# A new written-out order of all steps in a fused attention and gated-MLP kernel, and its PE fillers

## Chip, cores, metric

One core of one Trainium2 chip. The metric is device time in microseconds (us) of one execution, lower is better; what is given is the median of three runs.

## What is computed

Attention in chunks of 32 positions over 8 memory keys and a context of up to 56 neighbours, then a gated MLP with a spatial mix over the sequence:

```python
# q, k, v: 4 batches, 8 heads, 768 positions, 64 wide
for c in range(24):                                   # chunks of 32
    scores = scale * q_c @ concat(mem_k, k_ctx).T     # 8 + up to 56 keys
    a = softmax(scores)
    out[c] = a @ concat(mem_v, v_ctx)
x = out as (4, 768, 512)
h = gelu(x @ w_in)                                    # 512 -> 1024
u, v = halves of h
v_n = (v - mean) / sqrt(var + 1e-6) * g_ln
v_s = w_sg @ v_n + b_sg                               # over the 768 positions
y = x + (u * v_s) @ w_out                             # 512 -> 512
```

## The kernel before

The whole kernel is some 1,100 small named steps. Each is defined once (`step(name, does, engine)`, line 184) and issued by the loop at lines 490 to 495 in the order of the names in the table `ORDER` (line 31). Every engine's wrapper (`InOrder`, line 86) keeps program order, so that `ORDER` is at once the order of each engine's queue and that of the DMA issues, which all stand on SP's queue. A star behind a name takes the step's second engine. No planner runs here: what stands in the table is what happens.

The steps, by their names:
- `q`, `k`, `v` + unit: loads of an attention unit. A unit (0 to 23) is 128 positions of one batch with all 8 heads; q and k have two buffers, v three.
- `S` + unit (line 285): the scores, 32 matmuls of 64x32 by 64x64 in float32 into one of two PSUM halves. Then on DVE `mx` (row maximum), `sb` (subtract), on ACT `ex` (exp), on DVE `sm`, `sa`, `sr` (sum, add, reciprocal) and on DVE or POOL `nm` (normalise).
- `T` + unit (line 327): four 128x128 transposes; `p` copies them to SBUF (ACT or DVE).
- `A` + unit (line 341): attention times values, 32 float32 matmuls; `xc`, `xh`, `xl` copy the result and split it into a high and a low float32r part (ACT, then DVE or POOL).
- `ri`, `ro`, `d1` to `d9` (line 190): the weights w_in (8 pieces, half 1 before half 0) and w_out (4 pieces) arrive as 64-bit numbers and are turned into high and low parts on DVE, ACT and POOL; `g`, `ga`, `gb` do the same for w_sg from float32.
- `V` + batch and unit within the batch (line 396): the v half of x @ w_in for 128 positions, 12 matmuls of 128x128 by 128x512 (3 products of high and low parts over 4 blocks of 128). Then `v1` (gelu, ACT), `v5`, `vx`, `vy`, `v6` (statistics), `v7`, `v8`, `v9` (normalise and split).
- `U` + batch, half (384 positions) and block (line 431): 12 matmuls by 128x384 and the gelu `u1`. A `U` of half 0 needs the units 0 to 2 of its batch and the first four pieces of w_in's half 0.
- `W` (line 438): the spatial mix, 18 matmuls, needs all six `v9` of the batch; `w1`, `w2` shift and gate on DVE, `w3`, `w4` split again.
- `O` (line 456): 12 matmuls with w_out, needs four `w4` and the w_out parts; `o1` adds x, `out` stores.
- `zz` + n: n filling matmuls of 128x128 on the identity into a free PSUM tile (`warm`, line 486); nothing reads them.

PE's products go to one of four PSUM tiles (mma to mmd), taken at the matmul and given back by the step that reads them. So the S and A steps of the units, 48 in all and needed by the V and U steps of their batch, are spread between the large products. Batch 0 is the start-up: its V, U and W come in the first 125 us, while the weights are still being made. From 200 us on the order is nearly all large products.

Of the kernel before, what the change touches and what calls it, by code (L numbers as in the profile page):

```python
# [32 lines left out]
zz8 q2 sb0 d9i11 mx1 ex0 k2 z0 sb1 sm0 ex1 sa0 sm1 k3 sr0 sa1 nm0 sr1 d2i12 q3 T0 nm1 d4i12 p0* T1 ri03 d2i13 p1
A0 d1i12 d4i13 d1i13 d6i12 A1 zz9 d3i12 ri01 d6i13 d3i13 d5i12 xh0 xh1 d5i13 v3 xc0 d2i10 xc1 d7i13 xl0 d4i10 v4
d1i10 d8i13 d6i10 g11 d3i10 d9i13* d7i12* S2 zz2 g30 d5i10 d8i12 mx2 g41 d7i10 xl1 S3 zz3 k4 d9i12 sb2 d8i10 mx3
ex2 q4 d9i10* sb3 V01 sm2 ex3 q5 d1i03 sa2 d1i01 d3i03 sr2 sm3 nm2* d3i01 k5 V00 d1i00 sa3 d5i01 ri02 v101 sr3
d2i00 g31 nm3 d3i00 g21 d4i00 d2i03 d5i00 g20 T3 d4i03 T2 d6i00 p3 g40 p2* d7i00 v100 A3 g10 d6i03 d8i00 S4 ro0
d2i01 xc3 d9i00 v501 A2 d4i01 v6 mx4 xh3 d6i01 S5 zz2 xh2 xl3 sb4 xc2 q6 xl2 k7 mx5 d7i01 V02 q7 ex4 k6 d2i02
d8i01 v5 d1i02 sm4 d4i02 cb d9i01* d3i02 d6i02 V03 sa4 d5i02 sr4 sb5 d7i02 v102 nm4 vx01 d5i03 T4 ex5 p4* d8i02
z5 d7i03* A4 d9i02 sm5 d8i03 vy01 S7 v502 xc4 v7 sa5 v601 S6 xh4 d9i03* k9 sr5 q9 xl4 mx7 ga41 U000 k8 ga40 mx6  # L40
q8 ga11 nm5* sb7 ga10 ga20 sb6 ex7 gb10 U001 ex6 v701 ga21 g00 ga30 gb40 sm7 v801 vx02 V04 ga31 gb30* z6 g51
gb41 sa7 gb31 sm6 g50 u1001 sr7 vy02 sa6 nm7* u1000 S9 v901* v602 T5 k11 S8 p5 q11 gb11 sr6 mx9 v104 k10 U003
nm6 ga00 q10 ga51 gb21 mx8 g01 ga50 sb9 gb00 sb8 T7 v504 T6 gb20 ex9 A5 p6 v702 ex8 gb50 sm9 S11 v8 xc5 p7* S10
v802 q13 sm8 xh5 k13 v902 A7 mx11 k12 ga01 q12 A6 xl5* v10 gb01 u1003 v9 U010 xc6 sa8 sb11 xc7 sr8 v103 sa9 vx04
nm8 sr9 U013 vy04 mx10 nm9* ex11 gb51* v604 sb10 z11 V05 sm11 v704 u1010 sa11 v500 sr11 d2o0 vx00 nm11* vy00
v503 ex10 T9 T8 v600 v804 p9* S12 p8 sm10 v904 d4o0 S13 k14 mx12 q14 A9 sa10 mx13 k15 q15 v700 A8 v12 sb13 u1013
v105 vx03 sr10 sb12 v800 nm10* v11 U002 vy03 v505 v603 d6o0 vx05 v703 ex13 T11 vy05 v900* ex12 v605 T10 p11* S14
v803 z12 xc9 v705 S15 k16 xc8 v903 mx14 q16 v805 U011 mx15 k17 p10 sm12 q17 v905 sb15 sa12 sm13 W013 u1002 sr12
d1o0 nm12* sa13 sb14 ex15 d3o0 sr13 sm15 ex14 W010 nm13 d5o0 sa15 sm14 d7o0 ro1 u1011 sr15 w1013 nm15* d8o0 W000
sa14 d9o0 w2013 sr14 w1010 nm14 d2o1 d1o1 d4o1 w2010 W012 d3o1 w1000 d6o1 d5o1 w2000 d7o1 ro2 w3000 w4000* T13  # L50
d8o1 T12 w1012 S17 d9o1* S16 mx17 q19 k19 A11 mx16 q18 sb17 k18 A10 xc11 v14 sb16 d2o2 v13 W001 p12* d1o2 ex17
d3o2 z17 sm17 d4o2 d5o2 xc10 p13 U012 sa17 d6o2 ex16 sr17 w1001 d7o2 ro3 nm17 d8o2 W002 w2001 w3010 d9o2* w4010
sm16 u1012 sa16 d1o3 w3001 d2o3 d3o3 w2012 T15 T14 d4o3 w4001* T17 d5o3 w3012 A12 w3013 w1002 w4013 A13 p14 v15
w4012* S19 p15 v16 w2002 d6o3 S18 w3002 q21 mx19 w4002 k21 W003 q20 mx18 k20 sb19 sb18 ex19 d7o3* ex18 sr16 d8o3
z18 nm16* W011 sm18 w1003 d9o3 sa18 w2003 sm19 w3003 S21 sr18 w4003 w1011 S20 q23 nm18 k23 O003 w2011 k22 mx21
q22 w3011 mx20 w4011* O001 sb21 o1003 ex21 sa19 out003 sr19 sm21 nm19* O000 sa21 o1001 sr21 out001 nm21* O010
o1000 out000 O013 o1010 out010 O012 o1013 out013 O011 o1012 out012 O002 o1011 xh11 xh10 out011 xl11* xh9 xl10
V15 o1002 xh7 xl9 xh6 out002 xh8 xl7* xl6* V11 xl8* v115 xc12 xc13 U103 v111 v511 vx11 vy11 v611 U111 u1103 v711
v811 v911* V14 u1111 V10 v114 v514 vx14 vy14 v614 v714 A14 v110 v814 v510 T18 xc14 v17 v914 T16 vx10 vy10 T19
sb20 S23 v610 p16* S22 ex20 mx23 A15 sm20 mx22 A16 xc15 v18 p17* sb22 A17 p18 v19 sa20 v710 ex22 sr20 sb23 v20  # L60
V13 nm20* p19 sm22 xc17 xc16 sa22 sr22 v810 nm22 ex23 v910 U112 z23 sm23 v113 v513 U100 u1112 sa23 vx13 sr23
vy13 nm23 v613 v713 v813 T20 T22 u1100 v913 T21 A18 A19 p20* v21 p21* v22 V12 U101 v112 v512 vx12 vy12 v515 v612
U102 u1101 v712 v812 vx15 vy15 v615 v912* U110 u1102 v715 v815 v915* U113 u1110 W102 u1113 W100 w1102 w2102
w3102 w4102* W101 w1100 w2100 w3100 w4100 W103 w1101 w2101 w3101 w4101* W111 w1103 w2103 w3103 w4103 W113 w1111
w2111 w3111 w4111 W110 w1113 w2113 w3113 w4113* O100 w1110 w2110 w3110 w4110* O103 o1100 out100 W112 o1103
out103 O102 w1112 w2112 w3112 w4112 O101 o1102 out102 O111 o1101 xh14 xh12 out101 xl14 xh13 xl12* O110 o1111
xl13 out111 xc19 xc18 O112 o1110 out110 V21 o1112 out112 O113 v121 v521 vx21 vy21 v621 V20 o1113 xh17 v721 xh16
out113 xl17* xh15 xl16* v821 xl15 V24 v120 v921* v520 vx20 vy20 v620 V22 v124 v720 v524 v820 vx24 v920 vy24 V25
v624 v122 v724 v522 v824 vx22 v924* vy22 v622 U211 v125 v722 v525 v822 vx25 v922* U212 u1211 vy25 v625 v725 v825
A20 u1212 v925* A21 xc20 p22* v23 xc21 V23 U201 v123 v523 vx23 vy23 v623 U200 u1201 v723 v823 v923* U203 u1200  # L70
W210 u1203 W203 w1210 U202 w1203 w2203 U213 u1202 w3203 w4203* W202 u1213 U210 w1202 w2202 w3202 w4202* W212
u1210 w2210 w3210 w4210* W211 w1212 w2212 w3212 w4212 W213 w1211 w2211 w3211 w4211 W200 w1213 w2213 w3213 w4213*
W201 w1200 w2200 w3200 w4200* T23 w1201 A22 p23 w2201 A23 w3201 xc22 w4201 xc23 O213 O202 o1213 out213 O201
o1202 out202 O211 o1201 out201 O203 o1211 out211 O200 o1203 out203 O212 o1200 xh19 xh20 out200 xl19 xh18 xl18*
O210 o1212 xl20 out212 V31 o1210 xh23 xh21 out210 xl23* xh22 xl21 xl22* V32 v131 v531 vx31 vy31 v631 v731 V33
v132 v831 v532 v931 vx32 vy32 v632 U310 v133 v732 v832 v932* V35 u1310 U303 v135 v535 vx35 vy35 v635 V34 u1303
v735 v835 v935* V30 v134 v534 vx34 vy34 v634 v734 U313 v130 v834 v530 v934 vx30 vy30 v533 U300 u1313 v630 v730
v830 vx33 vy33 U301 v633 u1300 v930* v733 v833 U311 v933 u1301 W301 u1311 W303 w1301 w2301 W313 w1303 w2303 U302
w1313 w2313 U312 u1302 w3303 w3301 w4303* w4301* W300 w3313 u1312 w4313 W311 w1300 w2300 w3300 w4300 W312 w1311
w2311 w3311 w4311 W302 w1312 w2312 w3312 w4312* W310 w1302 w2302 w3302 w4302* O301 w1310 w2310 w3310 w4310 O302  # L80
o1301 out301 O310 o1302 out302 O313 o1310 out310 O311 o1313 out313 O312 o1311 out311 O300 o1312 out312 O303
# [477 lines left out]
```

## Time and profile before

| | us |
|---|---|
| median of three runs (lowest, highest) | 414.51 (411.21, 415.73) |
| the profiled execution's own time | 411.95 |
| its span, first to last instruction | 410.0 |
| granted clock of PE, mean of the span | 0.971 |

| engine | busy us | share | instructions |
|---|---|---|---|
| PE (matmuls) | 381.1 | 93% | 4862 |
| DVE | 223.7 | 55% | 440 |
| ACT | 160.1 | 39% | 267 |
| POOL | 101.6 | 25% | 112 |

Busy time is what an engine's instructions cover. PE's weight loads (PEld) stand in a row of their own and run beside its matmuls. A wait called "issue" is idle time for which the profile shows no other engine or transfer that ended it. Every step is recorded through one helper, so all rows have its line, L94; steps are told apart by the names of their tiles.

### The profile page before, as it was taken

How to read it: one execution, taken by the hardware profiler on the slowest of the kernel's cores; microseconds unless marked ns; L12 is line 12 of the kernel's file. 1: busy time of each engine (PE TensorE's matmuls, PEld its weight loads, DVE VectorE, ACT ScalarE, POOL GpSimd, SP SyncE). 2: the span in 40 equal slices, each digit the busy share in tenths (PEclk: the TensorE clock that was granted, in tenths of full speed). 3: DMA queues.
4: the chain of work that ended last, by engine and by line, in shares of the span. 5: the costliest groups of instructions: out<-in, count | busy, mean ns of one | idle time of the engine just before them, and what ended most of it. 6: DMA issues, size and time to landing. Idle time of an engine off the chain costs nothing.

```text
span 410.0 us, 10958 instructions
## 1 busy us (share of the span) xinstructions
PE 381.1 (93%) x4862; PEld 357.5 (87%) x4862; DVE 223.7 (55%) x440; ACT 160.1 (39%) x267; POOL 101.6 (25%) x112
## 2 busy tenths in 40 slices
...
GB/s 285 407 395 243 190 235 202 230 112 245 64 270 76 212 199 77 2 73 137 105 1 2 6 71 74 5 54 0 0 2 2 98 58 2 0 0 2 0 62 93
DMA packets 19151, 43.96 MB, mean 107 GB/s; under 512 B 2592, under 2 KB 8224, under 8 KB 19104
## 3 DMA queue, kind: packets, MB, share of 16 engines
...
q8 instruction: 38, 0.62, 0.6%
...
HBM read 36.96 MB, written 6.29 MB: 105 GB/s over the span
## 4 chain that ended last, share of the span: by engine, by line
PE 87%; DVE 4%; issue 4%; ACT 2%; DMA 2%; SPq 0%
PE mmc L94 21%; PE mma L94 21%; PE mmd L94 18%; PE mmb L94 16%; PE av L94 6%; PE s L94 4%; DMA kb<-in_ks 2%; DVE ea L94 1%; SPq L94 0%; DVE paira L94 0%; DVE eb L94 0%; ACT L94 0%; DVE w_in_lo L94 0%; ACT pt L94 0%; ACT xa L94 0%
## 5 line engine op out<-in xcount | busy, mean ns | idle before, releaser
...
L94 DVE SCALAR_TENSOR_TENSOR mmd<-mmd,g_all,b_all 128x384 f32<-128x384 f32 x10 | 6.2, 624 | 21.2 <-PE mmd L94 21.2
L94 PE MATMUL s<-kb,qb 64*32 64x64 f32 x768 | 11.5, 232 | 6.6 <-issue 5.2
L94 PEld LDWEIGHTS s<-kb,qb 64*32 64x32 f32 x768 | 9.0, 109 | 8.7 <-issue 6.4
L94 PE MATMUL s<-ka,qa 64*32 64x64 f32 x768 | 11.5, 239 | 5.5 <-issue 3.0
L94 PEld LDWEIGHTS s<-ka,qa 64*32 64x32 f32 x768 | 9.2, 112 | 6.8 <-issue 3.8
L94 PE MATMUL av<-pt,vb 64*64 64x32 f32 x512 | 10.7, 231 | 4.0 <-issue 3.2
L94 DVE SCALAR_TENSOR_TENSOR mmc<-mmc,g_all,b_all 128x384 f32<-128x384 f32 x9 | 5.6, 618 | 15.4 <-PE mmc L94 15.4
L94 PEld LDWEIGHTS av<-pt,vb 64*64 64x64 f32 x512 | 9.6, 147 | 4.8 <-issue 3.8
L94 PE MATMUL av<-pt,vc 64*64 64x32 f32 x512 | 10.3, 229 | 2.7 <-issue 2.0
L94 PEld LDWEIGHTS av<-pt,vc 64*64 64x64 f32 x512 | 9.4, 145 | 4.0 <-issue 2.9
L94 PE MATMUL mmc<-w_in_hi,paira 128*128 128x512 f32 x40 | 11.9, 423 | 0.8 <-DVE paira L94 0.8
L94 PE MATMUL av<-pt,va 64*64 64x32 f32 x512 | 10.2, 229 | 2.5 <-issue 1.9
L94 PEld LDWEIGHTS av<-pt,va 64*64 64x64 f32 x512 | 9.3, 146 | 3.5 <-issue 2.4
L94 POOL TENSOR_TENSOR rsb<-rsb,mhalf 128x1 f32<-128x1 f32 x8 | 4.7, 588 | 26.7 <-DVE rsb L94 26.7
L94 DVE SCALAR_TENSOR_TENSOR mma<-mma,g_all,b_all 128x384 f32<-128x384 f32 x8 | 4.9, 616 | 11.3 <-PE mma L94 11.3
L94 PE MATMUL mmc<-paira,w_out_hi 128*128 128x384 f32 x56 | 10.9, 336 | 0.0
L94 PEld LDWEIGHTS mmc<-w_in_hi,paira 128*128 128x128 f32 x40 | 7.9, 202 | 2.7 <-DVE paira L94 1.0
L94 PEld LDWEIGHTS mmc<-paira,w_out_hi 128*128 128x128 f32 x56 | 9.8, 188 | 0.0
L94 PE MATMUL mma<-pairb,w_in_hi 128*128 128x384 f32 x48 | 9.3, 336 | 0.0
L94 POOL TENSOR_TENSOR rsc<-rsc,mhalf 128x1 f32<-128x1 f32 x8 | 4.8, 597 | 18.3 <-DVE rsc L94 17.2
L94 POOL TENSOR_TENSOR pairb<-uf,pairb 128x384 fp32r<-128x384 f32 x2 | 2.3, 1145 | 27.3 <-ACT pairb L94 27.3
...
## 6 DMA issues: line engine op xcount, KB each, us to landing
...
```

The source lines that it names most:

```text
L94: return self.tc.keep_in_program_order(getattr(self.engine, name)(*args, **kw))
```

## The change

Only two things differ: the table `ORDER`, nearly every row of it, and with it the places and counts of the `zz` steps. The same steps are issued, each once.

```diff
-ri11 k0 q0 q1 k1 v0 v1 zz5 ri12 d2i11 ri13 d1i11 d4i11 d3i11 v2 d6i11 d5i11 ri10 S0 zz2 d7i11* ri00 mx0 d8i11 S1
...
+q0 k0 k1 ri11 q1 v1 ri12 zz2 ri10 ri13 v0 S0 zz5 mx0 ri01 sb0 ex0 d2i11 q2 d1i11 z0 d4i11 S1 zz6 k2 sm0 d3i11
...
```

The fillers are `zz5 zz2 zz8 zz9 zz2 zz3 zz2` before, 31 matmuls, the last two of them behind S5, and `zz2 zz5 zz6 zz7 zz4 zz6` now, 30 matmuls, the last six ahead of the first V. Some steps take their other engine. DVE loses four nm (8 are left), one xl and one d9 of w_out to POOL, and takes four gb (6), three w4 (20), two d7, one d9 of w_in and one v9 from it, 5 instructions more in all. The step d9o3, the last of w_out, goes from POOL to DVE. ACT has 24 table loads for 22.

Three places show how the rows move. First PE in the start-up, from the transposes of units 2 and 3 to the third V. `s<-` is an S, `av<-` an A, `mm<-ident,e` a T, `mm<-w_in,pair` a V. Before:

```order
L94 MATMUL mma<-ident,ed 128x128 x4
L94 MATMUL mmb<-ident,ec 128x128 x4
L94 MATMUL av<-pt,va 64x32 x32
L94 MATMUL s<-ka,qa 32x64 x32
L94 MATMUL av<-pt,vc 64x32 x32
L94 MATMUL s<-kb,qb 32x64 x32
L94 MATMUL mmc<-ident 128x128 x2
L94 MATMUL mmc<-w_in_hi,paira 128x512 x4
L94 MATMUL mmc<-w_in_lo,paira 128x512 x4
L94 MATMUL mmc<-w_in_hi,paira 128x512 x4
```

Now:

```order
L94 MATMUL av<-pt,vc 64x32 x32
L94 MATMUL mma<-ident,ed 128x128 x4
L94 MATMUL s<-ka,qa 32x64 x32
L94 MATMUL mmb<-w_in_hi,paira 128x512 x4
L94 MATMUL mmb<-w_in_lo,paira 128x512 x4
L94 MATMUL mmb<-w_in_hi,paira 128x512 x4
L94 MATMUL av<-pt,va 64x32 x32
L94 MATMUL mmd<-w_in_hi,paira 128x512 x4
L94 MATMUL mmd<-w_in_lo,paira 128x512 x4
L94 MATMUL mmd<-w_in_hi,paira 128x512 x4
L94 MATMUL s<-kb,qb 32x64 x32
L94 MATMUL mmc<-ident,ea 128x128 x4
```

Before, four steps A3, S4, A2 and S5 stand in a row, and two fillers and then V02 follow. Now A2 and S4 stand ahead of V01, A3 alone between V01 and V02, and S5 and T4 behind V02.

Second, DVE up to the last part of w_in that the first U waits for (`w_in_lo<-`, the last row in each). `m`, `ex` and `raw` are a weight piece on its way, `e`, `mx`, `rd` a unit's softmax, `st`, `mv`, `rs` the statistics of a v tile. Before, these are DVE's instructions 72 to 82:

```order
L94 TENSOR_TENSOR eb<-s,mxc 128x512
L94 TENSOR_TENSOR ea<-ea,rdb 128x512
L94 BN_AGGR mvb<-stb 128x2
L94 SCALAR_TENSOR_TENSOR mb<-rawb,mb 128x512
L94 COPY pt<-mmb 128x4x128
L94 TENSOR_TENSOR mb<-mb,exb 128x512
L94 TENSOR_REDUCE rdc<-eb 128x8
L94 TENSOR_SCALAR rsb<-mvb 128x1
L94 BN_STATS stc<-gc 128x6
L94 TENSOR_SCALAR rdc<-rdc 128x8
L94 TENSOR_TENSOR w_in_lo<-mb,w_in_hi 128x512
```

Now they are its instructions 63 to 73:

```order
L94 RECIPROCAL rdb<-rdb 128x8
L94 TENSOR_TENSOR w_in_lo<-mf,w_in_hi 128x512
L94 TENSOR_TENSOR pairb<-xb,pairb 128x4x128
L94 SCALAR_TENSOR_TENSOR me<-rawe,me 128x512
L94 SCALAR_TENSOR_TENSOR exa<-rawa,exa 128x512
L94 TENSOR_TENSOR me<-me,exe 128x512
L94 TENSOR_TENSOR ma<-ma,exa 128x512
L94 TENSOR_REDUCE mxc<-s 128x8
L94 COPY pt<-mmc 128x4x128
L94 TENSOR_TENSOR eb<-s,mxc 128x512
L94 TENSOR_TENSOR w_in_lo<-me,w_in_hi 128x512
```

The statistics (`BN_STATS`, `BN_AGGR`, `rsb`) and a normalisation of softmax that stood ahead of the last row stand behind it now, and the row itself stands nine instructions earlier. It belongs to piece 03 before and to piece 00 now.

Third, PE around the first run of S and A steps between U products. Before, with units 5 to 11:

```order
L94 MATMUL mmc<-ident,ed 128x128 x4
L94 MATMUL mmb<-ident,ec 128x128 x4
L94 MATMUL av<-pt,vc 64x32 x32
L94 MATMUL s<-kb,qb 32x64 x32
L94 MATMUL s<-ka,qa 32x64 x32
L94 MATMUL av<-pt,vb 64x32 x32
L94 MATMUL av<-pt,va 64x32 x32
L94 MATMUL mmb<-pairb,w_in_lo 128x384 x4
L94 MATMUL mmb<-pairb,w_in_hi 128x384 x8
```

Now, with units 5, 6, 9 and 10:

```order
L94 MATMUL mmc<-ident,eb 128x128 x4
L94 MATMUL mmd<-paira,w_in_lo 128x384 x4
L94 MATMUL mmd<-paira,w_in_hi 128x384 x8
L94 MATMUL av<-pt,vc 64x32 x32
L94 MATMUL mmb<-ident,ec 128x128 x4
L94 MATMUL s<-kb,qb 32x64 x32
L94 MATMUL s<-ka,qa 32x64 x32
L94 MATMUL mmc<-w_in_hi,pairb 128x512 x4
L94 MATMUL mmc<-w_in_lo,pairb 128x512 x4
L94 MATMUL mmc<-w_in_hi,pairb 128x512 x4
```

Five steps in a row (A5, S11, S10, A7, A6) were between U003 and U010. Now A5, a T, S9 and S10 stand between U003 and V04, with A6, S11 and S12 behind the U011 that follows.

## Rows read from the trace of the kernel before

**Rows 1.** The page: busy us, share and instructions of each engine.

```profile
PE 381.1 (93%) x4862; PEld 357.5 (87%) x4862; DVE 223.7 (55%) x440; ACT 160.1 (39%) x267; POOL 101.6 (25%) x112
```

**Rows 2.** Stretches: length, busy us (instructions) of each engine, clock, DMA share, GB/s.

```profile
core 0: us, PE busy (x) PEld busy (x) DVE busy (x) ACT busy (x) POOL busy (x), PEclk, DMA share, GB/s
0.00:53.85 53.85, 40.18 (x962) 33.37 (x962) 41.69 (x82) 32.17 (x51) 15.53 (x22) 0.97 0.80 291
0.00:66.50 66.50, 52.83 (x1154) 44.57 (x1154) 52.58 (x102) 43.22 (x71) 27.78 (x35) 0.97 0.80 285
0.00:99.48 99.48, 80.14 (x1931) 70.02 (x1932) 74.98 (x153) 67.22 (x107) 42.30 (x50) 0.93 0.74 255
0.00:142.73 142.73, 120.19 (x2747) 108.79 (x2747) 110.96 (x223) 90.45 (x142) 56.71 (x64) 0.94 0.66 227
0.00:198.65 198.65, 173.18 (x3487) 157.46 (x3487) 139.43 (x281) 111.77 (x177) 68.85 (x77) 0.94 0.55 189
198.65:406.57 207.92, 207.89 (x1377) 199.99 (x1376) 83.67 (x158) 48.30 (x90) 32.76 (x35) 1.00 0.09 30
```

**Rows 3.** PE's waits: waiter and releaser, us in total, times, longest.

```profile
PE s L94 <- issue: 8.2, 5, 2.2
PE av L94 <- issue: 7.2, 4, 2.0
PE s L94 <- DMA qa<-in_qs: 2.5, 1, 2.5
```

**Rows 4.** The chain that ended last, 42 to 73 us: start, us, what.

```profile
42.73 4.60 PE mmc L94 x12
...
62.45 0.93 PE s L94 x62
...
67.95 2.23 issue
...
72.62 1.40 issue
```

**Rows 5.** Timeline of PE, 18 to 41 us: start, us, instruction, count [wait before].

```profile
18.05 2.27 PE L94 MATMUL mmc<-ident 128*128 128x128 f32 x18
...
37.28 0.32 PE L94 MATMUL s<-ka,qa 64*32 64x64 f32 x8 [1.31 <-issue]
37.53 1.14 PE L94 MATMUL av<-pt,vc 64*64 64x32 f32 x64
38.59 0.78 PE L94 MATMUL s<-kb,qb 64*32 64x64 f32 x55
41.00 0.32 PE L94 MATMUL s<-kb,qb 64*32 64x64 f32 x9 [1.63 <-issue]
```

**Rows 6.** The page: instruction packets (count, MB, share), and a group of S matmuls.

```profile
q8 instruction: 38, 0.62, 0.6%
...
L94 PE MATMUL s<-kb,qb 64*32 64x64 f32 x768 | 11.5, 232 | 6.6 <-issue 5.2
```

**Rows 7.** The chain again, 52 to 132 us: one step of each kind.

```profile
52.48 1.44 PE s L94 x94
...
56.22 2.08 PE mmc L94 x12
...
65.66 0.44 PE mmc L94 x4
...
77.11 3.96 PE mmb L94 x12
...
83.17 2.78 PE mmd L94 x12
...
99.48 3.12 PE mmb L94 x18
...
129.77 2.00 PE av L94 x128
```

**Rows 8.** Stretches of lower granted clock: the longest, and all four summed.

```profile
70.50:80.74 10.24, 8.84 (x232) 8.47 (x213) 5.11 (x13) 5.11 (x8) 3.01 (x4) 0.50 0.73 231
...
sum 23.89, PE 21.81 PEld 19.73 DVE 13.73 ACT 15.14 POOL 5.39; mean PE 5.45 PEld 4.93 DVE 3.43 ACT 3.78 POOL 1.35
```

More of the change, by code (lines that the diff above doesn't have):

```diff
@@ L31 @@
 ORDER = """
-ri11 k0 q0 q1 k1 v0 v1 zz5 ri12 d2i11 ri13 d1i11 d4i11 d3i11 v2 d6i11 d5i11 ri10 S0 zz2 d7i11* ri00 mx0 d8i11 S1
[L33 to L81, printed above, removed]
@@ L82 @@
-o1300 out300 o1303 out303
+q0 k0 k1 ri11 q1 v1 ri12 zz2 ri10 ri13 v0 S0 zz5 mx0 ri01 sb0 ex0 d2i11 q2 d1i11 z0 d4i11 S1 zz6 k2 sm0 d3i11
+d6i11 sa0 mx1 v2 sr0 d5i11 nm0* sb1 q3 ex1 d2i12 T0 zz7 d1i12 d4i12 sm1 k3 p0 d6i12 d3i12 sa1 d7i11* ri03 sr1
+d1i13 d8i11 nm1* d3i13 d1i10 ri00 A0 d9i11* d3i10 d5i13 T1 xh0 d5i10 g20 p1 xl0 xc0 v3 A1 d2i13 d2i10 d4i13
+d5i12 g01 S2 zz4 d4i10 d6i13 xh1 d7i12 xc1 v4 d6i10 d8i12 g40 d7i13 mx2 S3 zz6 k4 d7i10* d8i13 d9i12 sb2 d8i10
+mx3 q4 ex2 d9i13* d9i10 sm2 k5 sb3 q5 d2i03 ex3 V00 sa2 d1i01 d4i03 sr2 sm3 nm2* ri02 d3i01 g30 d2i01 sa3 d1i03
@@ new lines @@
+d4i01 sr3 d5i01 T2 d3i03 g50 nm3* p2 g51 A2 d2i00 d5i03 g00 T3 xl1 v100 S4 v5 d6i03 p3 d4i00 d6i01 V01 ro0 xh2
+d7i03 mx4 xc2 k6 xl2 d7i01 d8i03 sb4 d9i03* q6 A3 d2i02 g10 d1i02 ex4 cb d6i00 d3i02 V02 v6 sm4 xc3 d5i02 d8i01
+sa4 d1i00 xh3 sr4 d9i01* d3i00 nm4* d4i02 S5 xl3* T4 q7 d5i00 k7 V03 v102 d6i02 v101 d7i00* d7i02* d8i00 mx5
+d8i02 p4* S6 d9i02 sb5 A4 q8 d9i00* k8 ex5 mx6 ga00 z5 v7 U001 xc4 sm5 gb00 ga01 sb6 xh4 g11 sa5 v502 ex6 xl4
+U002 ga30 sr5 v501 ga10 nm5 ga40 z6 ga51 gb10 sm6 ga50 vx01 ga20 vx02 S7 sa6 gb50 vy01 vy02 v500 S8 q9 sr6 mx7
@@ new lines @@
+nm6* k9 T5 mx8 u1001 q10 u1002 k10 v602 U003 sb7 ga11 gb20 sb8 p5* gb11 g31 vx00 A5 ex7 gb30* g41 ex8 gb51 vy00
+sm7 g21 T6 xc5 v8 sm8 S9 v600 p6* v601 S10 q11 mx9 k11 u1003 sa7 mx10 V04 k12 xh5 q12 sb9 ga41 xl5 ga21 sa8 sr7
+sb10 nm7* U011 sr8 ex9 v701 ex10 nm8* ga31 v801 gb41* A6 v901 sm10 S11 v9 u1011 v700 S12 xc6 sa10 q13 mx11 v103
+k13 T7 sm9 v800 q14 T8 mx12 p7 k14 v900 V05 p8* sb12 v104 sb11 v503 gb40* A7 vx03 ex12 sr10 v504 nm10* ex11 A8
+v10 xc7 gb31* z11 z12 sm11 xc8 v11 U013 vx04 gb21* sa11 vy04 sa9 sr11 v604 v702 sr9 nm11* vy03 v802 S14 gb01*
@@ new lines @@
+v603 S13 k16 nm9 q16 U010 v902* u1013 q15 sm12 k15 v105 v703 mx13 v803 U012 v505 u1010 v903 mx14 vx05 v704 vy05
+d1o0 T9 v804 v605 sa12 T10 d2o0 p9 T11 sb13 d3o0 A9 p10* d4o0 v705 A10 v12 v904* sr12 p11* v13 U000 ex13 nm12
+xc9 sm13 v805 sb14 xc10 v905 A11 sa13 d6o0 S16 v14 u1012 sr13 d5o0 S15 q18 nm13* mx16 k18 W000 q17 mx15 ex14 ro1
+d7o0 sb15 k17 sm14 sa14 sr14 u1000 nm14* d8o0 W010 w1000 d9o0 w2000 ex15 w3000 sm15 xc11 w4000 T12 T14 p12 sa15
+d2o1 T13 d1o1 d4o1 A12 sb16 d3o1 d6o1 S17 ex16 v15 d5o1 p14 S18 k19 w1010 ro2 d7o1* W001 k20 mx18 d8o1 q20 mx17
@@ new lines @@
+q19 d9o1 sb18 sb17 ex18 w2010 ex17 z18 W013 sm16 w3010 z17 w1001 w4010* w2001 d1o2 w3001 d2o2 d3o2 sr15 w4001*
+W002 d4o2 w1013 nm15* d5o2 d6o2 w2013 ro3 d7o2* W003 w3013 w1002 d8o2 w4013* d9o2 w2002 sm18 w3002 sa16 w4002*
+W011 sr16 d1o3 w1003 d3o3 nm16 d5o3 w2003 d2o3 w3003 p13* S19 d4o3 w4003* S20 q21 d6o3 k21 w1011 W012 d7o3 k22
+mx19 q22 w2011 d8o3 sm17 w3011 d9o3* w4011* O002 sa17 sa18 w1012 sr17 sr18 w2012 nm17* w3012 nm18 O000 o1002
+w4012 mx20 out002 O001 o1000 out000 O003 o1001 out001 O010 o1003 xh6 xh8 out003 xl6* xh7 xl8 O011 xl7* o1010
@@ new lines @@
+xc12 out010 O012 o1011 out011 V12 o1012 out012 T18 v112 T16 T15 v512 T17 sb20 A13 sb19 ex20 A14 vx12 xc13 p15*
+v16 ex19 sm20 A15 v17 xc14 p16* sa20 sm19 p17 v18 V10 sr20 vy12 sa19 nm20 v612 sr19 v712 nm19 v812 v912* O013
+v110 v510 S22 xh9 o1013 xh11 S21 vx10 xl9* out013 xh10 xl11 mx22 k23 U100 mx21 q23 sb22 xl10 sb21 ex22 V15 vy10
+xc15 v610 sm22 ex21 v710 sa22 sm21 sr22 sa21 nm22* sr21 u1100 A17 v115 nm21 v810 A16 v515 xc17 v20 v910* S23 p18
+v19 vx15 vy15 v615 xc16 mx23 V14 v715 v815 v915* U113 v114 V13 u1113 U101 v113 v513 vx13 vy13 v613 V11 u1101
```

21 lines of the change are left out of this document (added).

## Prediction

> **What bounds the kernel now.** I read the page first: in a span of 410.0 us PE is busy 381.1 us, against 223.7 for DVE and 160.1 for ACT [rows 1]. Only PE's lost time can pay. The busy times by stretch tell where that lies: from 198.65 us on PE is busy 207.89 of 207.92 us, so no order gains there; by 198.65 us it has been idle for 25.5 us, and in the same stretch its granted clock is 0.94 [rows 2]. By 53.85 us (start of the first U) DVE has been busy 41.69 of 53.85 us, and PE waits for the weights and the softmax that DVE prepares. Later PE is ahead of DVE.
>
> The list of PE's waits is headed by "issue": 8.2 + 7.2 = 15.4 us in nine waits, up to 2.2 us each; no other releaser has over 2.5 us [rows 3]. Eight of the nine stand on the chain that ended last, 13.7 us in all; two pieces of it are shown, 2.23 and 1.40 us [rows 4]. The reader is to see in the timeline where they fall. One ends at 37.28 us; then come 8 S, 64 A and 55 S matmuls and the next, which ends at 41.00 [rows 5]. That is 127, and with the weight loads and two bare waits 256 instructions. The pair that ends at 70.18 and 74.02 [rows 4] has the same distance. The page shows where 256 comes from: queue q8 brought 38 instruction packets of 0.62 MB, 16 KB each, and PE's 4862 matmuls with their 4862 loads are 38 times 256 [rows 1, 6]. So PE's program comes in blocks of 256 instructions, and PE stands still when it has used up one before the next is in.
>
> **What a block costs.** From one edge to the next took 41.00 - 37.28 = 3.72 and 74.02 - 70.18 = 3.84 us [rows 4, 5], though 128 small matmuls take 2.0 us (two A: 2.00 us, two S: 1.44 [rows 7]). With more loads in flight it took longer: by the count the edge before 70.18 lies in the S at 62.45, 19 matmuls before its end, at 63.0 and so 7.2 us earlier [rows 4]; that block's own work is 4.2 us. I take 3.8 us where loads are few and 4.4 where they are many, the nearest rows being the two pairs; 7.2 is the upper end. A block of less work stalls for the difference. An S or an A has 32 matmuls in the program but 64 in the trace (12 S steps make x768 [rows 6]), so one is 128 instructions and two in a row fill a block.
>
> The Trainium skill ("Runtime: NRT & Kernel Launch", section "Instruction fetch mechanics") says that such a crossing is "mostly hidden". By that rule the waits would have another cause and an order with other blocks would leave them as they are. The trace disagrees: two of the waits take 1.31 and 1.63 us [rows 5], one 2.23 [rows 4], at a spacing of 256 instructions.
>
> **What the change does to the edges.** All eight waits of before lie 194 or 195 instructions past a multiple of 256, counted from PE's first. I laid the same ruler on the new order (S and A 128, V, U and O 24, W 36, T 8 instructions, a filler 4, bare waits 1). The new order has no four S or A steps in a row, but two and three remain, and each such group can still hold a whole block. Blocks with almost nothing but S and A:
> - before: A2/S5, S10/A7, A9/A8, A11/A10, A13/S19, S22/A15, A16/A17 (seven);
> - now: S9/S10, S16/S15, A14/A15, A16/S23 (four, 2.0 to 2.1 us of work each). A7/A8, A20/A21 and A22/A23 fill blocks as well, but 8 to 28 slow matmuls stand queued before these, which give the fetch 1.4 to 5 us more (0.17 us each, a U's 2.08 over its 12); I cost them at 0.3, 0 and 0.
>
> Four mixed blocks now have 3.8 to 4.1 us of work (ending in A5, T8/V05, S13 and A11) and one 3.2 (ending in W001): at 4.4 they cost 0.4 to 0.6 each, and 1.2. Sum now: 2.3 + 2.4 + 1.9 + 1.9 for the four, 0.3 + 1.9 + 1.2 for the others, 11.9 us against 13.7. So as an antidote to the waits the change is worth about 2 us: the fill is cut by half of what it would take.
>
> The clock hangs on these waits. Four stretches, 23.89 us together, ran at a granted 0.50 (1.2 GHz) [rows 8]; three of them begin within 1.4 us of the end of an issue wait, the longest at 70.50 behind the wait that ended at 70.18. A V at 42.73 us took 4.60 us instead of 2.78, the U at 77.11 us 3.96 instead of 2.08 [rows 4, 7]: some 1.8 us a slow step, and the longest stretch holds two steps' worth. Seven full blocks gave three drops; four give one to two: 2 to 3 us less.
>
> The fillers are 30 now and 31 before, all ahead of the first V in the new order. Nothing comes from their number.
>
> **The early stage.** Ahead of the first U DVE has 82 instructions in 41.69 us (0.508 each); in the new order 73. At the same idle time the first U starts 9 x 0.508 = 4.6 us earlier, at 49.3. I check with PE's work done by then, steps at full clock (S 0.72, A 1.0, T 0.44, V 2.78, U and O 2.08, W 3.12 us [rows 7], a filler 0.25, nine taking 2.27 [rows 5]): 31.8 us before, 30.9 now. I keep the books as time beyond PE's work: 53.85 - 31.8 = 22.0 before, 49.3 - 30.9 = 18.4 now. The new order of the first loads (q, k, k ahead of the first weights) starts S0 earlier, at most by the 2.5 us that PE waited for qa [rows 3], but DVE gets its first weights later by about as much, and S1 waits for the same bytes; I cost it at nothing, between a gain and a loss of 2.5 us.
>
> **Stage by stage**, time beyond PE's work:
> - A5. DVE ahead of it: 102 instructions and 52.58 us by 66.50 before (22.9 beyond), 94 now, 48.5 us of work. With 12.8 us of DVE's idleness (12.2 by the first U, 13.9 by 66.50 before) A5 starts at 61.3; PE's work is 39.0: 22.3. The early gain is nearly spent here, since the new order brings PE less work by A5.
> - First U of the second half. Before U010 at 77.11 [rows 7]: 29.0, after two waits (3.6) and the clock. Now U011, with one full block (2.3) and 0.7 for the clock: 25.3.
> - First W. Before 99.48 [rows 7]: 33.7. Now A7 to S16 add 3.8 for edges, 1.5 for the clock, 0.5 for a wait on ACT: 31.1, which with 70.4 us of PE's work is 101.5 us. DVE then has 158 instructions, at 74.98 / 153 = 0.49 each 77.4 us: 24.1 idle, as before (24.5).
> - First O. Before 142.73: 39.3. Now PE needs 30.2 us from W to O and 2.1 for an edge and the clock, 32.3. DVE has 60 instructions to do by then; at before's pace in this stage (43.25 us / 70 = 0.618) these are 37.1 us, at their busy time (35.98 / 70 = 0.514) 30.8. I take 33.5, nearer to PE's own 32.3: 34.4.
> - To A18/A19. Before + 7.0 (198.65 us: 46.3). Now two full blocks 3.8, clock 1.7, T and A waits 1.0: 40.9. From there to the last matmul before + 0.8, the same now: 41.7, against 47.1 before (406.57 us less 359.5 us of PE's work).
>
> So some 5.3 us less: span 404.7, and the profiled execution, whose own time stands 1.95 us over its span, 411.95 - 5.3 = 406.6. The runs' median is 414.51, 2.6 above that one, so I forecast 414.5 - 5.3 = 409.2 us, 1.3% less. About 1% is what a measurement here can tell from no change.
>
> **Rivals.**
> A, DVE or the old waits keep the bound: from first W to first O DVE needs its 37.1 us (+3.6), or the waits don't follow the blocks and stay at 13.7 us (+1.8, so 411.0). For it: DVE is busy 83% in that stage already [rows 2], and the last of the w_out steps (d9o3) is DVE's now, POOL's before. Against: before, PE was late there by itself. Time 409.2 + 3.6 = 412.8, within 1%. Chance 0.30, of which 0.05 for the waits that stay.
> B, slower: the seven blocks of 2.0 to 4.1 us between A5 and W001 fall in the stage with the heaviest loads (mean DMA share 0.80 up to 66.50 us, still 0.66 up to 142.73 [rows 2]), and their fetches come late. Each 0.1 us on an edge there costs 0.7 us. At 5.7 us an edge instead of 4.4: 7 x 1.3 = 9.1, and with one clock drop more (1.8): 409.2 + 10.9 = 420.1. For it: one edge took 7.2. It decides from 5.5 us an edge on (418.7 is +1%). Chance 0.15.
> C, the first U's 4.6 us are kept whole (DVE idles less after it, since V's and U's stand earlier) and the clock drops once only: 409.2 - 3.5 - 2.5 = 403.2. For it: DVE's idleness from 53.85 on is waiting for PE. Chance 0.13. The forecast itself: 0.42, own range 405 to 413.
>
> **How the numbers follow.** Faster by over 1% (below 410.4): C whole, nine tenths of the forecast's lower and middle part (0.36) and 0.03 of A: 0.52. Slower by over 1%: B, 0.15. Within 1%: 0.33. The range holds 8 in 10 from 401, below C, to 419, where B begins to count: most of B and the low end of C lie outside.
>
> **What would show it.** Right: issue waits at S10, S15/S16, A14/A15 and A16/S23, 3.5 to 4.5 us from edge to edge, their sum 10 to 13; the first U near 49 us, A5 near 61, the first W near 101, the first O near 135. Wrong: issue waits under 6 us in all (then blocks aren't what stalls PE or the ruler has moved), a first U after 52 us (DVE idles more in the new order), or PE idle on DVE between first W and first O for over 4 us (A), or edges of 6 us and more between 60 and 110 us (B).

## The result and the profile after

The changed kernel takes 401.25 us (median of four runs, 400.00 to 405.11), the kernel before 415.07 beside it (411.21 to 415.73): a ratio of 0.9701, 95% interval 0.9611 to 0.9792, so 13.8 us or 3.0% less. The profiled execution took 400.69 us over a span of 398.8, against 411.95 over 410.0 before.

The page, first its busy times, where [rows 1] stood, and its instruction packets, where [rows 6] did:

```profile
PE 377.5 (95%) x4860; PEld 353.2 (89%) x4860; DVE 226.0 (57%) x445; ACT 162.9 (41%) x269; POOL 98.4 (25%) x107
...
q8 instruction: 38, 0.62, 0.7%
```

The work is the same but for one filler, and so are the 38 packets. The span has lost 11.2 us: PE is busy 3.6 us less, and idle 7.6 us less. The list of PE's waits, where [rows 3] stood:

```profile
PE s L94 <- issue: 6.3, 5, 2.1
PE av L94 <- ACT xa L94: 2.4, 2, 1.7
PE s L94 <- DMA ka<-in_ks: 2.0, 1, 2.0
PE av L94 <- issue: 1.8, 1, 1.8
```

"Issue" fell from 15.4 us in nine waits to 8.1 in six and still stands at the head of the list. On the chain that ended last (start, us, what), where [rows 4] stood, it has five pieces of over 0.4 us:

```profile
21.39 1.14 issue
...
61.56 1.28 PE s L94 x89
62.85 1.57 issue
...
76.28 1.98 PE av L94 x123
78.26 1.82 issue
...
95.86 1.39 PE s L94 x92
97.25 2.10 issue
99.78 4.66 PE mma L94 x18
...
167.52 2.00 PE av L94 x128
169.52 0.70 PE s L94 x48
170.23 1.18 issue
```

Together 7.8 us, against 13.7. Each piece cuts into a row of S or A matmuls, and each lies 194 or 195 instructions past a multiple of 256 from PE's first: in S10, A8, S15 and S23 behind the first U and in S2 ahead of it.

The trace also holds the transfers of queue q8, so that what ends such a wait can be read. By the count of its instructions PE passes the border before the wait in S10 at 60.53 us, and it goes on at 64.42. The DMA view (queue, kind: packets, MB, share of 16 engines) of the windows 60.53 to 62.00, 62.00 to 63.10 and 63.10 to 64.42:

```profile
q1 hardware_dynamic: 298, 0.54, 100.1%
...
q1 hardware_dynamic: 217, 0.31, 87.2%
q8 instruction: 1, 0.02, 5.6%
...
q1 hardware_dynamic: 116, 0.34, 91.4%
```

One instruction packet is brought in this time. It starts at 62.04, takes 0.99 us, and PE goes on 1.4 us after it has landed. At all five pieces a packet landed 1.2 to 1.5 us before the wait ended.

The W at 99.78 took 4.66 us where one at full clock took 3.12 [rows 7]. The stretches of half clock, where [rows 8] stood (columns as in [rows 2]):

```profile
20.67:27.50 6.83, 5.70 (x142) 4.89 (x138) 5.11 (x6) 3.39 (x6) 5.39 (x4) 0.50 1.02 379
34.33:37.74 3.41, 3.41 (x94) 2.75 (x87) 2.83 (x5) 2.81 (x6) 1.49 (x1) 0.50 0.53 149
99.18:102.59 3.41, 3.24 (x15) 3.07 (x15) 2.69 (x5) 3.37 (x5) 0.00 (x0) 0.50 0.90 253
sum 13.65, PE 12.35 PEld 10.71 DVE 10.64 ACT 9.57 POOL 6.88; mean PE 4.12 PEld 3.57 DVE 3.55 ACT 3.19 POOL 2.29
```

Now 13.7 us against 23.9, and only one stretch lies behind the first U; it begins where the wait of 97.25 ends. Behind the first U is where most was won. The stretch from the first U to the last matmul, first before, then now:

```profile
53.85:406.54 352.69, 340.89 (x3906) 324.09 (x3900) 181.41 (x358) 127.89 (x217) 86.08 (x90) 0.97 0.24 80
```

```profile
50.75:395.35 344.60, 336.19 (x3964) 318.60 (x3964) 184.72 (x371) 130.00 (x219) 81.26 (x86) 1.00 0.25 82
```

The first U came 3.1 us earlier, and the stretch behind it is 8.1 us shorter, though PE's work in it, at full clock, is 0.8 us more.

### The profile page after: what moved, and what is told of

Read it like the earlier page. It is cut to its first block, busy times and chain, and to the rows that moved or that the text cites. A ratio compares the mean times of both kernels' runs of the same rounds, so it can differ in the third digit from the quotient of the medians.

```text
span 398.8 us, 10975 instructions
## 1 busy us (share of the span) xinstructions
PE 377.5 (95%) x4860; PEld 353.2 (89%) x4860; DVE 226.0 (57%) x445; ACT 162.9 (41%) x269; POOL 98.4 (25%) x107
## 4 chain that ended last, share of the span: by engine, by line
PE 87%; DVE 5%; ACT 4%; issue 2%; DMA 1%; SPq 0%; ACTq 0%
PE mmb L94 22%; PE mmd L94 21%; PE mmc L94 20%; PE mma L94 14%; PE av L94 5%; PE s L94 4%; DMA rawb<-in_w_in 1%; ACT w_sg_hi L94 1%; ACT L94 1%; DVE w_in_lo L94 0%; DVE ma L94 0%; DVE mb L94 0%; DVE exb L94 0%; DVE rda L94 0%; DVE eb L94 0%
## 5 line engine op out<-in xcount | busy, mean ns | idle before, releaser
L94 PE MATMUL s<-ka,qa 64*32 64x64 f32 x768 | 11.8, 245 | 4.7 <-issue 2.7
L94 PE MATMUL s<-kb,qb 64*32 64x64 f32 x768 | 11.8, 240 | 4.1 <-issue 3.6
L94 DVE SCALAR_TENSOR_TENSOR mmb<-mmb,g_all,b_all 128x384 f32<-128x384 f32 x10 | 6.2, 624 | 9.5 <-PE mmb L94 9.5
L94 PE MATMUL mmd<-w_in_hi,paira 128*128 128x512 f32 x40 | 11.1, 400 | 0.0
L94 PE MATMUL mmb<-pairb,w_in_hi 128*128 128x384 f32 x56 | 10.9, 337 | 0.0
L94 PE MATMUL mmb<-paira,w_in_hi 128*128 128x384 f32 x56 | 10.9, 337 | 0.0
L94 PE MATMUL av<-pt,vb 64*64 64x32 f32 x512 | 9.0, 220 | 1.7 <-ACT xa L94 1.7
L94 PEld LDWEIGHTS av<-pt,vb 64*64 64x64 f32 x512 | 8.2, 135 | 2.7 <-ACT xa L94 1.9
L94 DVE TENSOR_REDUCE mxa<-s 128x8 f32<-128x512 f32 x8 | 5.5, 685 | 8.4 <-PE s L94 8.4
L94 PEld LDWEIGHTS mmb<-paira,w_in_hi 128*128 128x128 f32 x56 | 9.8, 188 | 0.0
L94 PEld LDWEIGHTS mmb<-pairb,w_in_hi 128*128 128x128 f32 x56 | 9.8, 188 | 0.0
L94 DVE SCALAR_TENSOR_TENSOR mmd<-mmd,g_all,b_all 128x384 f32<-128x384 f32 x7 | 4.4, 624 | 9.5 <-PE mmd L94 9.5
```

What stands on the lines that cost most here:

```text
L94: return self.tc.keep_in_program_order(getattr(self.engine, name)(*args, **kw))
```

## The experiments

The theory: PE's instructions arrive in blocks of 256, and PE stands still at a block's border where the block behind it held little but S and A matmuls. Which blocks those are hangs on where the borders fall, so a few instructions put ahead of PE's first step move every border and must move, bring or remove waits, with the order of the steps untouched. The rivals: the order itself gives the gain (what DVE, the loads or the queues do), the waits following it only by chance; the fillers or the clock give it. In the diffs below, long lines end behind the place that matters.

**Borders moved by 180 instructions, slow padding.** 45 tiny matmuls, which nothing reads, ahead of PE's first step; one of these is two matmuls and two loads, so 180 instructions. (In all padded kernels the helper stands on line 92.)

```diff
-q0 k0 k1 ri11 q1 v1 ri12 zz2 ri10 ri13 v0 S0
+q0 k0 k1 ri11 q1 v1 ri12 pp45 zz2 ri10 ri13 v0 S0
...
+    def pad(n):
+        for _ in range(n):
+            tensor.matmul(mms.free[0][0:32, 0:64], ident[0:64, 0:32], ident[0:64, 0:64], start=True, stop=True)
```

> The new order with 45 tiny matmuls on the identity (180 instructions) put ahead of PE's first filler, where PE waits for its first q and k anyway; all else as in the new order. Blocks theory: the edges of the 256-instruction blocks move by 180 and every block then holds enough slow matmuls; the issue waits at S10, A8, S15 and S23 go, issue after 45 us sums to under 1 us (7.2 in the new order), no stretch of half clock after 45 us, and the time falls by 6 to 9 us to 392 to 395. Rival (the waits belong to the steps: a run of S and A steps stalls by itself): the same four waits at the same steps, 401 us within 2.

Measured: 400.17 us (397.14 to 400.80), ratio 0.9715 (0.9629 to 0.9801). The waits went as the border theory had it, 0.8 us left on the chain; from first U to last matmul it took 337.8 us instead of 344.6. But the time, 392 to 395 us by the expectation, hardly fell, for a reason of the padding's own, in PE's timeline (start, us, instruction, count):

```profile
1.39 10.96 PE L92 MATMUL mma<-ident 64*32 64x64 f32 x94 [1.39 <-POOL mhalf L92]
12.27 1.19 PE L92 MATMUL s<-ka,qa 64*32 64x64 f32 x64
```

The padding took 11 us, some 0.12 us a matmul, and S0 began at 12.27 us instead of 4.61. So the first U came at 57.42.

**By 20 instructions.** The same with `pp5`.

> The new order with 5 such tiny matmuls (20 instructions) ahead of the first filler. Blocks theory: edges move by 20 instructions, waits come 20 instructions earlier, at S10, S15, S23 and A15 as before, and two blocks that were mixed become full, which puts new waits at T8 (or in S12 just ahead of it) and S18, 1.7 to 2.3 us each; issue after 45 us 9 to 12 us, time 2 to 4 us above the new order: 403 to 405. Rival (the waits belong to the steps): as the new order, 401 within 2.

Measured: 405.69 us (402.05 to 408.30), ratio 0.9835 (0.9728 to 0.9941), a little above what was expected. The chain behind the first U:

```profile
65.24 1.33 issue
...
75.42 0.96 issue
...
81.36 1.17 issue
86.44 1.09 issue
...
100.46 2.34 issue
...
114.90 1.82 issue
...
175.23 1.09 issue
```

Seven waits, 9.8 us, where there were four, 6.7. New are the pieces at 75.42 (T8), 86.44 (S13) and 114.90 (S18); T8 and S18 were foretold, the piece foretold at A15 is not there. Twenty instructions that compute nothing cost 4.4 us by the medians and 3.3 in the stretch from first U to last matmul (347.9 for 344.6). The intervals of the two ratios overlap, so the times alone don't show this cost; the waits do.

**The order before, by 208 and by 108 instructions.** `pp52` and `pp27` ahead of the first filler of before.

> The kernel before with 52 tiny matmuls (208 instructions) ahead of the first filler. Blocks theory: five waits instead of seven beyond the start-up, in A7, A8, S18, A15 and A17; none in S5, A10, S19; issue after 45 us falls from 12.1 to about 9, and the time by 3 to 5 us: 410 to 412. Rival: eight waits where they were, 415 within 2.

> The kernel before with 27 tiny matmuls (108 instructions) ahead of the first filler. Blocks theory: nine waits, in S5, S6, S10, A6, A9, A11, W003, S22 and A16; issue after 38 us 16 to 19 us, and the time 3 to 6 us above the kernel before: 418 to 421. Rival: eight waits where they were, 415 within 2.

Measured: 417.95 us (416.46 to 420.71), ratio 1.0170 (1.0079 to 1.0260), and 417.17 us (414.72 to 418.18), ratio 1.0133 (1.0028 to 1.0238). Both missed in time, the first by 6 us. The padding held S0 up to 15.04 us in the one and 9.70 in the other, against 6.36. The waits moved, mostly to the foretold steps. In the first they stand at A7, A8, S18 and A15, with one at W001 that was not foretold and none at A17; in the second at S6, S10, A6, A9, A11, W003 and A16, with 0.4 us in S5 and none in S22. The wait at W003 is put down to ACT by the profile for PE's matmul, but PE's load beside it shows the same wait as issue:

```profile
141.98 0.34 PE L92 MATMUL mmc<-w_sg_hi,vha 128*128 128x384 f32 x1 [3.71 <-ACT ec L92]
141.98 0.19 PEld L92 LDWEIGHTS mmc<-w_sg_hi,vhb 128*128 128x128 f32 x1 [3.60 <-issue]
```

It ends at residue 194, and an instruction packet landed 1.3 us before.

**By 180, quick padding.** The same 45 matmuls, with the two halves of PE's rows and several places in PSUM in turn.

```diff
     def pad(n):
-        for _ in range(n):
-            tensor.matmul(mms.free[0][0:32, 0:64], ident[0:64, 0:32], ident[0:64, 0:64], start=True, stop=True)
+        for i in range(n):
+            r, c = i % 2, (i // 2) % 4
+            at = 64 * ((i // 8) % 8)
+            tensor.matmul(
+                mms.free[r][CH * c:CH * c + CH, at:at + 64], ident[64 * r:64 * r + 64, 0:CH],
+                ident[64 * r:64 * r + 64, 0:64], start=True, stop=True,
+            )
```

> As e1, but the 45 tiny matmuls take the form and the places of an S step (two halves of the array and two PSUM tiles by turns), so that they should take 1.7 us instead of 11 and end before q and k land. Blocks theory: S0 starts by 5 us as in the new order, issue after 45 us stays under 1.5 us as in e1, no half clock after 45 us, and the time is 392 to 396 us. Rival (what e1 gained behind the start was only slack that its late start had left over): stalls gone as in e1, but the time does not fall, 398 to 402.

Measured: 394.98 us (394.23 to 396.19), ratio 0.9569 (0.9508 to 0.9631), as expected: 6.3 us under the changed kernel, and its slowest run is under the changed kernel's fastest (400.00). PE's waits and the stretch from first U to last matmul:

```profile
PE s L92 <- issue: 3.7, 3, 2.2
PE av L92 <- ACT xa L92: 3.3, 2, 2.6
PE av L92 <- ACT pt L92: 1.8, 2, 1.4
...
52.04:388.79 336.75, 334.01 (x3965) 316.57 (x3964) 185.25 (x371) 129.95 (x218) 81.05 (x86) 1.00 0.24 83
```

Two of the three issue waits of S steps lie ahead of 27 us (2.16 us at 9.04 and 1.06 at 25.60, both on the chain); the third, 0.48 us at 95.06, is the only piece of over 0.4 us behind the first U. In that stretch PE is busy 334.01 of 336.75 us.

**Half of each order.** The new order up to its first W and then the remaining steps in the old one's order; and the reverse.

```diff
 nm13* mx16 k18
-W000 q17 mx15 ex14 ro1
+u1000 mx15 k17 q17 sb15 W013
...
 sb15 sa12 sm13
-W013 u1002 sr12
+u1002 u1011 U012
```

> The new order up to its first W (all fillers and the whole start-up), then the remaining steps in the order of the kernel before. By the books (time beyond PE's work): 29.4 us at the first W as in the new order, then what the old order adds from there, 13.6 less one wait: 41 to 43 at the end, 405 to 408 us, issue waits at S10, A8, S15, then S19, A15, A17. If all of the gain came before the first W: 401 to 402. If all of it came behind: 411 to 413.

> The order of the kernel before up to its first W, then the remaining steps in the new order. By the books 33.7 us beyond PE's work at the first W, then 6.9 as in the new order and one wait more (S16) 1.9: 42 to 44 at the end, 406 to 409 us, issue waits in S5, A7, A8, then S16, W001, A15 and S23. If all of the gain came before the first W: 412 to 414. If all behind: 401 to 403.

Measured: 412.37 us (406.72 to 416.29), ratio 0.9934 (0.9883 to 0.9986), a miss; and 408.70 us (406.42 to 412.38), ratio 0.9887 (0.9841 to 0.9932), within what was expected. The first is the time that its expectation had for a gain that comes whole behind the first W; the second does not bear that out. The two gains add up to 1.8%, short of the 3.0% of the whole. That speaks against a gain that sits in one stage. More does not follow: a joint brings steps together that neither order puts side by side, and it moves the borders too.

**No fillers.** All `zz` out of the new order, 30 quick paddings in their stead, so that the borders stay.

```diff
-q0 k0 k1 ri11 q1 v1 ri12 zz2 ri10 ri13 v0 S0 zz5 mx0
+q0 k0 k1 ri11 q1 v1 ri12 pp30 ri10 ri13 v0 S0 mx0
```

> The new order without its 30 fillers; 30 tiny quick matmuls stand in place of the first two so that all block edges behind the start keep their places. If the fillers matter (they keep the clock up until the first V): S0 to A3 and the first V's run at the half clock, the first U starts 1 to 3 us later than 50.75, and the time is 402 to 404. If they don't: 400 to 402, edges and waits as in the new order either way (S10, A8, S15, S23).

Measured: 402.31 us (400.57 to 404.04), ratio 0.9744 (0.9676 to 0.9812): no change from 401.25 that a measurement here can tell, and waits at the same four steps. The time lies 0.3 us inside the range that was named for fillers that matter, but the sign named with it is not there: the first U came at 49.24 us, earlier than 50.75, and no half clock stands ahead of it. No gain by the fillers shows.

**The controls.** Four kernels run together: the new order with 64 quick paddings, a whole block, so that the borders stand as in the changed kernel; the old order with 52 quick ones; the new one without fillers and with 77 quick ones (a shift of 188); the new one with fillers and 47 (188 too).

```diff
-q0 k0 k1 ri11 q1 v1 ri12 zz2 ri10 ri13 v0 S0 zz5 mx0
+q0 k0 k1 ri11 q1 v1 ri12 pp64 zz2 ri10 ri13 v0 S0 zz5 mx0
...
-ri11 k0 q0 q1 k1 v0 v1 zz5
+ri11 k0 q0 q1 k1 v0 v1 pp52 zz5
...
-q0 k0 k1 ri11 q1 v1 ri12 zz2 ri10 ri13 v0 S0 zz5 mx0
+q0 k0 k1 ri11 q1 v1 ri12 pp77 ri10 ri13 v0 S0 mx0
...
-q0 k0 k1 ri11 q1 v1 ri12 zz2 ri10 ri13 v0 S0 zz5 mx0
+q0 k0 k1 ri11 q1 v1 ri12 pp47 zz2 ri10 ri13 v0 S0 zz5 mx0
```

> The new order with 64 padding matmuls of the quick kind (256 instructions) ahead of its first product: the borders of the 256-instruction blocks lie among the steps exactly where they lie without padding. If the place of the borders decides, the issue waits stand again at S10, A8 or S13, S15 and S23, together 6 to 9 us, and the time is 401 us within 2. If it is the padding itself that saved 6 us in the run with 45 of them (a warmer start, a later start of PE), the time is 393 to 396 and the waits are gone.

> The order before with 52 quick padding matmuls (208 instructions), which unlike the slow ones don't hold up the start. Block theory: issue waits at A7, A8, S18, A15 or A16 and W001, none at A10 and S19; first U near 54 us, and the time 3 to 4 us under that of before, 409 to 411 us. If the old order can't gain by a shift alone, no change within 1 us.

> The new order without any filling matmul, with 77 quick padding matmuls that put the block borders some 188 instructions along. Block theory: no issue wait over 1 us after the first U; the time is 393 to 396 us. If the filling matmuls are worth something once the waits are gone (a clock that falls in the start or behind it), the time is 397 us or more.

> The new order with its fillers and 47 quick padding matmuls (188 instructions): borders 8 instructions further than in the run with 45. Block theory: no issue wait over 1 us after the first U, time 393 to 396 us, the same as with 45 within 1 us. If the gain of that run hung on one lucky place, waits come back and the time is 398 us or more.

Measured, beside 414.12 us for the kernel before:
- a whole block: 402.00 us (401.24 to 404.86), ratio 0.9704 (0.9632 to 0.9777). The four waits are back:

```profile
64.29 1.30 issue
...
79.37 1.95 issue
...
99.30 1.44 issue
...
171.80 1.35 issue
```

So padding gives nothing by itself; the 6 us hang on where the borders fall.
- the old order, 208: 408.29 us (406.75 to 411.04), ratio 0.9850 (0.9787 to 0.9913), a little more gain than expected. The waits behind the first U moved (none at A10 and S19) but stayed in sum, 11.7 us on the chain for 10.8, the longest 2.88 us. The gain lies elsewhere: ahead of the first U 0.6 us of waits are left of 2.9, and it came at 51.65 us instead of 53.85; behind it half clock took 10.2 us instead of 20.5.
- no fillers, 188: 393.38 us (391.89 to 394.67), ratio 0.9482 (0.9426 to 0.9539), the best of all. The cores' view and the stretch behind the first U:

```profile
core 0: 390.4 us, clock 1.000
...
50.05:386.99 336.94, 334.66 (x3964) 317.02 (x3964) 183.43 (x371) 129.97 (x219) 80.95 (x86) 1.00 0.25 83
```

- fillers, 188: 395.48 us (394.87 to 397.63), ratio 0.9543 (0.9489 to 0.9598), as expected, but with one wait that was not. It fell in the profiled execution, the slowest of the four, in the chain:

```profile
93.29 1.14 PE av L92 x64
94.42 0.37 PE s L92 x29
94.80 2.73 issue
97.52 1.54 PE s L92 x97
```

By the count it is a border too, at residue 194, and the border before it lay at 90.31: 7.2 us from one to the next, as once before the change (62.97 to 70.18).

**All of the new order side by side.** PE's issue waits of over 0.4 us on the chain behind the first U, the stretch from first U to last matmul in the profiled execution, and the median, in us (the kernel before took 413.2 to 415.1 us beside these):

| new order with | waits | stretch | median |
|---|---|---|---|
| borders moved by 20 | 9.8 | 347.9 | 405.69 |
| nothing (the change) | 6.7 | 344.6 | 401.25 |
| borders in place, no fillers | 7.1 | 346.0 | 402.31 |
| borders moved by 256 | 6.0 | 345.0 | 402.00 |
| borders moved by 188 | 2.7 | 340.9 | 395.48 |
| borders moved by 180, slow padding | 0.8 | 337.8 | 400.17 |
| borders moved by 180 | 0.5 | 336.7 | 394.98 |
| borders moved by 188, no fillers | 0 | 336.9 | 393.38 |

From no waits to 9.8 us of them the stretch grows by 11.0: each microsecond of waiting goes with 1.1, the clock that falls behind some of them included. The order of the steps, fillers aside, is one and the same in all rows, so the order alone does not set the time. In the old order the relation does not hold so well: waits of 8.3 (by 208, slow padding), 10.8 (none), 11.7 (by 208, quick) and 13.2 us (by 108, with the 3.7 at W003) go with 350.0, 352.7, 351.0 and 354.2 us. But the order counts too: wherever the borders were put, the stretch took 336.7 to 347.9 us in the new order and 350.0 to 354.2 in the old one.

## Why the prediction was right or wrong

Faster was right. The range from 401 to 419 us held the time by 0.25 us, and that is luck: the forecast's own 405 to 413 did not hold it, and of its signs the sum of the waits (10 to 13 us) and the wait at A14/A15 failed. The size was not right: 5.3 us less were forecast, 11.3 came in the profiled pair (411.95 to 400.69) and 13.8 in the medians. The nearest of the cases was rival C, 403.2 us, with a chance of 0.13. By the prediction's own books, the time beyond PE's work:

| up to | before | forecast | now |
|---|---|---|---|
| first U | 22.0 | 18.4 | 19.9 |
| A5 | 22.9 | 22.3 | 20.9 |
| first U of the second half | 29.0 | 25.3 | 23.0 |
| first W | 33.7 | 31.1 | 29.4 |
| first O | 39.3 | 34.4 | 32.0 |
| A18 | 46.3 | 40.9 | 35.4 |
| last matmul | 47.1 | 41.7 | 36.3 |

**What bounds the kernel: right.** PE's lost time alone paid; the waits are block borders. The same order with its borders moved takes from 394.98 to 405.69 us, and a shift by a whole block changes nothing. The Trainium skill ("Runtime: NRT & Kernel Launch", section "Instruction fetch mechanics") has such crossings "mostly hidden". By their number that holds here, for of the changed kernel's 38 blocks five end in a wait of over 0.4 us on the chain. That the waits have another cause, as the prediction reads the page, the runs decide against.

**The early stage: the number nearly right, the step not.** The first U was forecast at 49.3 us and came at 50.75. It was to come 4.6 us earlier because DVE has nine instructions less ahead of it, "at the same idle time". DVE has 74 for 82 by then, but its busy time fell by 1.0 us only (41.69 [rows 2] to 40.68); the rest of the 3.1 us is idle time, 12.2 to 10.1:

```profile
0.00:50.75 50.75, 41.33 (x896) 34.63 (x896) 40.68 (x74) 32.90 (x51) 17.14 (x21) 0.90 0.86 308
```

That S0 would start earlier was cost at nothing; it did, at 4.61 instead of 6.36 us, and of the two waits in S4 and S5 (1.31 and 1.63 us [rows 5]) none is left on the chain. Which of these brought DVE its work sooner no run shows.

**From the first U to A5: wrong.** "The early gain is nearly spent here" took 3.9 us of new idleness; it was 1.0, and A5 began at 59.84, not 61.3. DVE did not idle while PE worked through the U's; it was busy 8.83 of 9.15 us there:

```profile
50.75:59.90 9.15, 8.81 (x172) 7.99 (x173) 8.83 (x23) 9.08 (x18) 8.26 (x10) 1.00 0.73 234
```

This half of rival C came true: what was won by the first U is kept.

**The price of a block border: a term that was mis-sized.** I had 11.9 us of waits on the chain against 13.7; it was 7.8, and 8.4 with the pieces of under 0.4 us. Term by term:

| block that ends in | forecast | on the chain |
|---|---|---|
| S10 | 2.3 | 1.57 |
| S15 | 2.4 | 2.10 |
| A15 | 1.9 | 0.09 |
| S23 | 1.9 | 1.18 |
| A8 | 0.3 | 1.82 |
| the four mixed blocks (A5, T8/V05, S13, A11) | 1.9 | 0.31, at S13 |
| W001 | 1.2 | 0.23 |
| in the start | none | 1.14 |

The largest piece is the rows of the mixed blocks and of W001, 3.1 us forecast and 0.5 measured. Their work is 3.2 to 4.1 us, and at 4.4 us from border to border each was to stall. By the count a border came after 3.88 us at S10 (60.53 to 64.42), 4.21 at S13, 3.77 at S15 (95.59 to 99.35), 3.28 at W001, 3.07 at A15 and 3.15 at S23; only at A8 it took 4.9 (75.19 to 80.08) and in S2, at the start, 5.8.

So one price for the whole stage was the mistake; that "with more loads in flight it took longer" is no mistake. The traces of all runs have 75 borders behind which PE's next instruction starts over 0.6 us after the one before it. At each an instruction packet landed 1.1 to 1.7 us before PE went on. What differs is when the packet starts: 0.1 to 5.1 us after the border before. Where the DMA engines' mean busy share from border to border was under 0.5, it started within 1.9 us; where it was 0.8 or more, after 1.2 to 5.1. The border of 7.2 us before the change is one of 15 that took 5.5 us or more, seven of them ahead of 30 us and eight between 60 and 98. Its packet is not in the window from 62.97 to 67.70 but in that from 67.70 to 68.80:

```profile
q1 hardware_dynamic: 624, 1.34, 90.9%
...
q8 instruction: 1, 0.02, 5.7%
```

The next piece is A15, which has its wait beside another, as PE's timeline shows:

```profile
152.65 1.11 PE L94 MATMUL av<-pt,vc 64*64 64x32 f32 x64
154.47 1.46 PE L94 MATMUL av<-pt,va 64*64 64x32 f32 x64 [0.70 <-ACT xa L94]
```

PE would have waited for ACT there anyway. Against this stands A8, where the queued slow matmuls, which I took for a head start of the fetch, did not save it.

**From first O to A18: the largest single miss.** Forecast 40.9 - 34.4 = 6.5 us beyond PE's work, measured 35.4 - 32.0 = 3.4. Of the two full blocks (3.8 us) one was hidden but for 0.09 us and one took 1.18 us, and the clock (1.7 us) did not fall there at all.

**The clock: right in direction, the term most under-sized.** Forecast 2 to 3 us less, from "four give one to two" drops. It was one behind the first U, and a short one: 3.41 us, with the W at 4.66 us for 3.12. The long stretch of 10.24 us [rows 8] is gone. I take each step behind the first U from its first matmul to the next step's, less PE's idle time, against its time at full clock: the steps that touch a stretch of half clock took 9.4 us more than that before (ten steps) and 1.9 now (two), so 7.5 less. Behind the first U the books then close: PE's idle time fell from 11.8 to 8.4 us, 3.4 less; the clock 7.5 less; the other steps took 2.1 us more over their time at full clock; from 25.3 to 16.4 us beyond PE's work is 8.9.

**The rivals.** A fell: between first W and first O, PE was busy 32.72 of 32.95 us, so DVE's 29.58 us of work lay beside PE's:

```profile
99.71:132.66 32.95, 32.72 (x480) 31.89 (x478) 29.58 (x59) 15.11 (x27) 8.86 (x9) 0.96 0.49 157
```

Its other half, the waits that stay at 13.7 us, fell with the 7.8. B fell: it decides from 5.5 us a border on, and between A5 and W001 no border that held PE up took that long in this run. Of C both halves came, one drop of the clock and the early gain kept, though that gain was 3.1 us and not 4.6. That the fillers count, which I cost at nothing, fell with the runs without them.

**What stays open.** Why the clock falls more often in the old order: with 9.8 us of waits the new one has a granted clock of 1.00 behind the first U, the old one with 10.8 has 0.97. That the drops are brought on by the waits is argued from their places (before, three begin within 1.4 us of a wait's end; now one does, and three waits behind the first U have none behind them), not shown. And what holds the start of an instruction packet for up to 5.1 us. Neither was tried.

One thing goes past the prediction. The new order breaks up the long rows of S and A steps, but with the borders where they fall, at residue 194, small matmuls still fill a block four times. With the borders moved by 180 to 188 they fill almost none, and then the new order gives 4.3 to 5.2% instead of 3.0%.
